# Two GpSimd splits moved behind other work, and a VectorE copy written as a reduce, in an attention and expert kernel

## The chip, the cores and the metric

The kernel runs on one core of a Trainium2 chip. The metric is the device time of one execution in microseconds. TensorE (PE in the profile), VectorE (DVE), ScalarE (ACT) and GpSimd (POOL) each work through their own list of instructions in order; SyncE (SP) and GpSimd issue the transfers.

## The reference

Attention over keys and values that are averaged in groups of 8 rows, and then a layer of experts, in which each row goes through one expert of 8:

```python
k_p = k.reshape(B, H, Sp, 8, D).mean(axis=3)          # B=8, H=8, S=576, D=64, Sp=72
v_p = v.reshape(B, H, Sp, 8, D).mean(axis=3)
attn = softmax(q @ k_p.T / 8)                          # 576 x 72 for each batch and head
x = (attn @ v_p).transpose(0, 2, 1, 3).reshape(B, S, 512)
...
# rows of a batch in order: a row takes its own best expert, or the expert of the row before it
e = argmax(x @ w_gate) if s == 0 or sigmoid(x @ w_local) < 0.5 else prev_e
out[b, s] = softmax(x @ w_gate)[e] * (relu(x[b, s] @ w1[e]) @ w2[e])   # w1 512x1024, w2 1024x512
```

## The kernel before

**Two stages.** The first stage does the attention in 20 units of up to 256 rows (four pairs of batches, five units each), and behind each pair the routing: which expert each row takes (a scan along the rows), and its place in a list of rows for each expert. Attention's rows go to the DRAM tensor `x_rows`, the lists to `ids`. The second stage works through blocks of 256 rows of one expert: it gathers the rows, turns them on TensorE, multiplies by `w1` (eight groups of matmuls for a block) and by `w2`, and scatters the result. Matmuls run on pairs of numbers: each weight is split into a high part (`w1h`, `w2h`: ScalarE's cast, L170 and L175) and a low part (`w1l`, `w2l`: the difference, L171 and L176).

**The order is written by hand.** `PLAN` and `PLAN_B` are lists of short words, each a step with a number; `do` emits the step's instructions. Every engine keeps its instructions in this order, so a step that moves in the list moves past others on each engine that it uses. Words that matter here:

- `w2:c` loads chunk c (a quarter of the 1024x512 `w2`, as 128x1024 numbers) of the most used expert, `p2:c` splits it: a cast on ScalarE (L175), then the difference on GpSimd (L176), or on VectorE where the word is `p2.d`. `p1:c` and `p1.d:c` do the same for `w1` (L170, L171).
- `T0:u`, `T1:u`, `T2:u` turn unit u's attention weights on TensorE (L500) into a buffer of the PSUM pool `ps_t`, which has two; `T0c` and so on copy it out on ScalarE (L354). The routing's transposes (L622) take buffers of the same pool.
- `v0:u` to `v2:u` multiply by the values (L542), `fr`, `fs` scale (L559 to L567), `fp`, `fd` write rows (L580, then a store on SP).
- `rA:n` begins the routing of pair n with small VectorE operations (L598 to L613, `ab` among them), `rT0` to `rT2` turn `ab` (L622), `rS0` to `rS2` scan (L627), `rL` multiplies (L636, L641), `rO` makes the counts (L646 to L650: the line that changes is L649), `rV` the places (L661 to L676).
- `il:0` and `il:1` load a list of rows, `ga:0` and `ga:1` gather them: a sum and a scaling on VectorE (L259, L260), a memset (L262) and two indirect DMAs (L266) on GpSimd. `X0`, `X1` turn the gathered rows (L278) and split them (L285, L286); `L1:n` is a first-layer group (L309, L311) into buffer `hp[n % 3]`, `h0` and `h1` its activation (L316, L317, L321, L322), `L2` the second layer (L333).

Of the kernel before, what the change touches and what calls it, by code (L numbers as in the profile page):

```python
# [12 lines left out]
ALU = mybir.AluOpType  # L13
AX = mybir.AxisListType
# [63 lines left out]
vc:19 v2c:12 ch:0 vm.a:22 fr:12 v0:11 v0c:11 sb:14 vc:20 T0:13 lk:14 v1:11 T0c:13 s:0 s:0 v1c:11 T1:13 v2:11 rR:1 er:0  # L78
T2:13 rV:1 vm.a:18 s:0 sc:15 T1c:13 rP:1 ex:14 T2c:13 vl:19 lq:17 w2:1 fp:12 lq:18 v2c:11 vt:18 kc:15 v0:13 fr:11
vm.a:19 T0:14 mx:15 vd:19 vc:18 T0c:14 s:0 fp:11 w1:3 vl:20 sb:15 vd:20 T1:14 vt:22 v1:13 w1:2 T1c:14 vc:22 vl:18  # L80
fd.p:12 s:0 fd:11 fs:11 lv:23 vd:18 vm.a:21 sc:17 fs:12 vt:21 s:0 kp:14 ex:15 s:0 s:0 v0c:13 p2:1 v1c:13 v2:13 lq:16
s:0 mx:17 sb:17 vc:21 v2c:13 p1.d:3 T0:15 w2:0 v0:14 fr:13 T0c:15 lq:19 vl:21 s:0 T1:15 v0c:14 s:0 fp.d:13 kc:14 T2:15
T1c:15 v1:14 v0:15 fs:13 v1c:14 fd:13 sc:16 fr:14 vd:21 vp.d:23 w1:1 T2c:15 ex:17 s:0 p1:2 fs:14 T0:17 v0c:15 fp:14
w1:0 T1:17 v1:15 vl:22 T0c:17 mx:16 T1c:17 v2:15 fd.p:14 T2:17 v1c:15 sb:16 il:0 vt:23 v0:17 vm.a:23 rA:2 vc:23 T2c:17
sc:18 v2c:15 ex:16 p2:0 fr:15 T0:16 vd:22 mx:18 rT0:2 vl:23 vd:23 rS0:2 v1:17 T0c:16 T1:16 v0c:17 sb:18 v2:17 fp:15
v1c:17 T1c:16 T2:16 rT1:2 fd.p:15 ga:0 fs:15 p1.d:0 v2c:17 fr:17 fp:17 v0:16 rS1:2 T2c:16 sc:19 ex:18 rT2:2 mx:19
v0c:16 rS2:2 v1:16 v1c:16 v2:16 rE:2 sb:19 v2c:16 T0:18 T0c:18 T1:18 rL:2 T2:18 T1c:18 fr:16 fs:17 ex:19 il:1 fd.p:17
fp:16 rO:2 fd:16 v0:18 rR:2 ga:1 T2c:18 fs:16 p1.d:1 X0:0 v0c:18 X0c:0 T0:19 v1:18 v1c:18 T0c:19 v2:18 X1:0 v2c:18
T1:19 rV:2 v0:19 fr:18 X1c:0 T1c:19 v1:19 v0c:19 fs:18 v1c:19
""")  # L90
PLAN_B = plan("""
# [13 lines left out]
def moe_attention(ctx: ExitStack, tc: tile.TileContext, q, q_st, k, v, v_st, w_gate, w1, w2, out):  # L105
    nc = tc.nc
# [230 lines left out]
    with ExitStack() as actx:  # L337
# [254 lines left out]
        state = {"acc": None}  # L592

        def finish(lg, pr):
            def small(name, w, dt=F32):
                return ap2.tile([P, NC, w] if w > 1 else [P, NC], dt, name=name)
# [5 lines left out]
            fr, rs = small("fr", 1), small("rs", 1)  # L602
# [41 lines left out]
            oh, cs = ohs[pr % 2], ap2.tile([P, E, NC + 1], F32, name="cs")  # L644
# [1 line left out]
            nc.vector.tensor_tensor(out=oc, in0=rt[:, 0:NC * E].rearrange("p (c e) -> p c e", e=E),  # L646
                                    in1=iota8[:, 0:1, :].broadcast_to([P, NC, E]), op=ALU.is_equal)
            if pr:
                nc.vector.tensor_copy(out=oh[:, :, 0], in_=state["acc"])  # L649
            nc.vector.tensor_tensor_scan(out=cs.rearrange("p e c -> p (e c)"), data0=seg0.rearrange("p e c -> p (e c)"),  # L650
                                         data1=oh.rearrange("p e c -> p (e c)"), initial=0.0, op0=ALU.mult, op1=ALU.add)
            state["acc"] = cs[:, :, NC]
# [75 lines left out]
        qg, qT, kg, vg, sc, att, fin, rw, tr2, vl = {}, {}, {}, {}, {}, {}, {}, {}, {}, {}  # L728
        first1, first2, lgs, fr = {}, {}, {}, {}
# [12 lines left out]
        def do(name, n):  # L742
# [59 lines left out]
            elif op == "fd":  # L802
                drain(rw[n])
            elif op == "rA":
                fin[n] = finish(lgs[n], n)
                step(fin[n])
            elif op in RSTEPS:
# [403 lines left out]
```

## Time and profile before

| | |
|---|---|
| median of 3 runs | 634.63 us (634.58 to 635.76) |
| the profiled execution | 631.1 us, of which the span 629.4 us |
| TensorE busy | 607.2 us (96%) |
| VectorE busy | 403.6 us (64%) |
| ScalarE busy | 290.8 us (46%) |
| GpSimd busy | 285.2 us (45%) |

All times in the rows below count from the start of the span. An engine's busy share over the whole span says little here: the first stage and the second have different limits, and the change lies where one goes over into the other, at 115 to 160 us.

### The profile page before, as it was taken

The numbers are of one execution on the slowest core, as the hardware profiler recorded it, in microseconds if no ns is written. First come the engines' busy times: TensorE is split into PE (matmuls) and PEld (weight loads), VectorE is DVE, ScalarE is ACT, GpSimd is POOL, SyncE is SP. The second block draws the span as 40 slices with busy tenths as digits, with TensorE's granted clock in tenths as the row PEclk, the third lists the DMA queues.
The fourth block names the chain that finished last, engine by engine and source line by source line (L and its number), as shares of the span: only waits on it lengthen the run. The fifth ranks groups of instructions, "written<-read, shape, count | busy, mean of one in ns | idle before, by whom it ended". The sixth has DMA issues, their size and how long they took to land. (4 is left out here: it accounts for less than half of the span.)

```text
span 629.4 us, 14760 instructions
## 1 busy us (share of the span) xinstructions
PE 607.2 (96%) x3516; PEld 526.8 (84%) x3517; DVE 403.6 (64%) x976; ACT 290.8 (46%) x692; POOL 285.2 (45%) x478
## 2 busy tenths in 40 slices
PE   7999999989999999999999999999999999999992
PEld 6998989878887878888888888888888888888881
DVE  7899899998875515344763585779344494543582
ACT  3677777956432313233642363665132462322550
POOL 5586767875672233203425164426331163132172
PEclk9899999989999999999999999999999999999997
DMA  8998994845102562102542174559121173121011
GB/s 328 348 388 292 346 347 128 314 152 201 20 21 81 172 233 51 50 17 67 167 167 85 27 242 139 153 192 318 50 59 26 42 249 118 34 67 44 24 52 37
DMA packets 53959, 92.00 MB, mean 146 GB/s; under 512 B 30634, under 2 KB 30634, under 8 KB 53932
## 3 DMA queue, kind: packets, MB, share of 16 engines
q1 hardware_dynamic: 45420, 69.61, 33.3%
q0 software_dynamic: 8512, 22.07, 10.3%
q8 instruction: 12, 0.20, 0.1%
q14 instruction: 15, 0.12, 0.1%
HBM read 71.54 MB, written 22.21 MB: 149 GB/s over the span
## 5 line engine op out<-in xcount | busy, mean ns | idle before, releaser
L309 PE MATMUL hp<-x,w1h 128*128 128x512 f32 x364 | 130.4, 399 | 0.1
L333 PE MATMUL o_ps<-w2h,ht_h 128*128 128x512 f32 x312 | 124.0, 397 | 0.0
L333 PE MATMUL o_ps<-w2l,ht_h 128*128 128x512 f32 x312 | 122.0, 391 | 0.0
L311 PE MATMUL hp<-x,w1l 128*128 128x256 f32 x364 | 102.1, 280 | 0.0
L1069 POOL TENSOR_TENSOR vt_in<-idk,zf 128x2 f32<-128x2 f32 x20 | 8.9, 446 | 188.4 <-PE tp L278 178.2
L333 PE MATMUL o_ps<-w2h,ht_l 128*128 128x512 f32 x312 | 87.6, 390 | 0.0
L316 ACT COPY hs<-hp 128x256 f32<-128x256 f32 x91 | 33.5, 371 | 108.4 <-PE hp L311 99.0
L309 PEld LDWEIGHTS hp<-x,w1h 128*128 128x128 f32 x364 | 68.4, 188 | 17.0 <-DVE hs L317 0.4
L1049 DVE TENSOR_SCALAR ob<-o_ps,m_a 128x512 f32<-128x512 f32 x42 | 31.5, 750 | 64.8 <-POOL m_e L1058 30.7
L321 ACT ACTIVATE ht_h<-hs 128x256 fp32r<-128x256 f32 x136 | 57.1, 420 | 29.1 <-DVE hs L317 24.4
L311 PEld LDWEIGHTS hp<-x,w1l 128*128 128x128 f32 x364 | 68.7, 189 | 0.9
L333 PEld LDWEIGHTS o_ps<-w2h,ht_l 128*128 128x128 f32 x312 | 58.6, 188 | 12.8
L333 PEld LDWEIGHTS o_ps<-w2h,ht_h 128*128 128x128 f32 x312 | 58.6, 188 | 11.9
L542 PE MATMUL op<-vaug,aT 128*128 128x148 f32 (+4 forms) x448 | 67.2, 310 | 0.6 <-ACT osb L354 0.6
L333 PEld LDWEIGHTS o_ps<-w2l,ht_h 128*128 128x128 f32 x312 | 58.6, 188 | 10.9
L542 PEld LDWEIGHTS op<-vaug,aT 128*128 128x128 f32 (+1 forms) x448 | 61.2, 182 | 4.0 <-issue 1.3
L322 DVE SCALAR_TENSOR_TENSOR ht_l<-hs,ht_h 128x256 fp32r<-128x256 f32 x136 | 56.6, 418 | 7.4 <-ACT ht_h L321 7.2
L1060 POOL DMA_INDIRECT out<-ob,m_e x42 | 47.8, 1137 | 21.8 <-issue 21.2
L317 DVE TENSOR_TENSOR hs<-hp,hs 128x256 f32<-128x256 f32 x91 | 37.7, 422 | 27.5 <-ACT hs L316 26.2
L285 ACT CAST x<-tp 128x512 fp32r<-128x512 f32 x46 | 24.9, 589 | 52.2 <-PE tp L278 48.4
L302 POOL DMA_INDIRECT vt_in<-x_rows,idk x42 | 41.4, 985 | 12.0 <-issue 8.8
L679 POOL DMA_INDIRECT ids<-pm,pos x36 | 37.5, 1043 | 18.6 <-issue 8.3
(249 smaller groups left out, 1157.4 us busy)
## 6 DMA issues: line engine op xcount, KB each, us to landing
raw<-in_moe_w SPq DMA_DIRECT2D x48, 512.0 KB
kk<-in_k SPq DMA_DIRECT2D x16, 576.0 KB
qt<-in_q SPq DMA_DIRECT2D x16, 512.0 KB
vt_in<-in_v SPq DMA_DIRECT2D x16, 512.0 KB
x_rows<-xs SPq DMA_DIRECT2D x16, 512.0 KB
idp<-ids SPq DMA_DIRECT2D x176, 1.0 KB
vt_in<-in_v_st SPq DMA_DIRECT2D x8, 256.0 KB
vt_in<-in_moe_w SPq DMA_DIRECT2D x4, 512.0 KB
```

The lines of the kernel that those rows point to most:

```text
L302: nc.gpsimd.indirect_dma_start(out=xg[:, h, :], out_offset=None, in_=x_rows[0:NT + 1], in_offset=bass.IndirectOffsetOnAxis(ap=idk[:, h:h + ...
L309: nc.tensor.matmul(out=ps, lhsT=W1[0][:, kk, f * P:(f + 1) * P], rhs=xt[:, kk].rearrange("p i n -> p (i n)"), start=(kk == 0), stop=False, ...
L311: nc.tensor.matmul(out=ps[:, 0:2 * P], lhsT=W1[1][:, kk, f * P:(f + 1) * P], rhs=xt[:, kk, 0, :], start=False, stop=(kk == KD - 1), skip_g ...
L316: nc.scalar.copy(out=hb[:, 0, :], in_=ps[:, 2 * P:])
L317: nc.vector.tensor_tensor(out=hb[:, 1, :], in0=ps[:, 0:2 * P], in1=hb[:, 0, :], op=ALU.add)
L321: nc.scalar.activation(out=ht[0][:, f, :], in_=hb, func=AF.Relu)
L322: nc.vector.scalar_tensor_tensor(out=ht[1][:, f, :], in0=hb, scalar=0.0, in1=ht[0][:, f, :].bitcast(F32), op0=ALU.max, op1=ALU.subtract)
L333: nc.tensor.matmul(out=to[h], lhsT=ht[i][:, kk, h * P:(h + 1) * P], rhs=W2[j][:, kk, :], start=(n == 0), stop=(n == 3 * KF - 1))
L542: nc.tensor.matmul(out=out, lhsT=lhs, rhs=rhs if len(out.shape) == 3 else rhs.rearrange("p s x -> p (s x)"), start=all(x[0] != n for x in ...
L679: nc.gpsimd.indirect_dma_start(out=ids[u % 4].rearrange("t m w -> (t m) w"), out_offset=bass.IndirectOffsetOnAxis(ap=pos[:, u:u + 1], axis=0),
L1049: nc.vector.tensor_scalar(out=ob[:, h, :], in0=o_ps[h], scalar1=m_a[:, h, 1:2], scalar2=None, op0=ALU.mult)
L1060: return nc.gpsimd.indirect_dma_start(out=outv, out_offset=bass.IndirectOffsetOnAxis(ap=m_e[h][:, 0:1], axis=0), in_=ob[:, h, :], in_offse ...
```

## The change

Two words of the list stand elsewhere, and one VectorE instruction is another operation with the same result (a sum over an axis of length 1). The rest of the list is the same, only broken into lines differently.

```diff
-fd.p:12 s:0 fd:11 fs:11 lv:23 vd:18 vm.a:21 sc:17 fs:12 vt:21 s:0 kp:14 ex:15 s:0 s:0 v0c:13 p2:1 v1c:13 v2:13 lq:16
+fd.p:12 s:0 fd:11 fs:11 lv:23 vd:18 vm.a:21 sc:17 fs:12 vt:21 s:0 kp:14 ex:15 s:0 s:0 v0c:13 v1c:13 v2:13 lq:16 s:0
...
-sc:18 v2c:15 ex:16 p2:0 fr:15 T0:16 vd:22 mx:18 rT0:2 vl:23 vd:23 rS0:2 v1:17 T0c:16 T1:16 v0c:17 sb:18 v2:17 fp:15
-v1c:17 T1c:16 T2:16 rT1:2 fd.p:15 ga:0 fs:15 p1.d:0 v2c:17 fr:17 fp:17 v0:16 rS1:2 T2c:16 sc:19 ex:18 rT2:2 mx:19
...
-fp:16 rO:2 fd:16 v0:18 rR:2 ga:1 T2c:18 fs:16 p1.d:1 X0:0 v0c:18 X0c:0 T0:19 v1:18 v1c:18 T0c:19 v2:18 X1:0 v2c:18
...
+sc:18 v2c:15 ex:16 fr:15 T0:16 vd:22 mx:18 rT0:2 vl:23 vd:23 rS0:2 v1:17 T0c:16 T1:16 v0c:17 sb:18 v2:17 fp:15 v1c:17
+T1c:16 T2:16 rT1:2 fd.p:15 p2:0 ga:0 fs:15 p1.d:0 v2c:17 fr:17 fp:17 v0:16 rS1:2 T2c:16 sc:19 ex:18 rT2:2 mx:19 v0c:16
...
+rO:2 fd:16 v0:18 rR:2 ga:1 p2:1 T2c:18 fs:16 p1.d:1 X0:0 v0c:18 X0c:0 T0:19 v1:18 v1c:18 T0c:19 v2:18 X1:0 v2c:18
...
             if pr:
-                nc.vector.tensor_copy(out=oh[:, :, 0], in_=state["acc"])
+                nc.vector.tensor_reduce(out=oh[:, :, 0], in_=state["acc"].unsqueeze(2), axis=AX.X, op=ALU.add)
```

On GpSimd, around the first gather (`qt` is its destination, `xs` a unit's rows), the difference between the two orders reads:

```order
 L171 TENSOR_TENSOR w1l<-kt,w1h 128x1024
 L580 TENSOR_TENSOR xs<-osb,rr 128x256 x2
+L580 TENSOR_TENSOR xs<-osb,rr 128x512 x2
 L176 TENSOR_TENSOR w2l<-vt_in,w2h 128x1024
-L580 TENSOR_TENSOR xs<-osb,rr 128x512 x2
 L262 MEMSET qt 128x1024
 L266 DMA qt<-x_rows,idr_132 128x512 x2
```

The split of chunk 0 has moved past the rows of unit 15 and stands directly ahead of the memset of the first gather.

On GpSimd, behind the second gather, there is now the split of chunk 1, which stood among the scatters of pair 1's lists before:

```order
 L262 MEMSET qt 128x1024
 L266 DMA qt<-x_rows,idr_133 128x512 x2
+L176 TENSOR_TENSOR w2l<-vt_in,w2h 128x1024
 L924 MEMSET zf 128x2
 L924 MEMSET zf_2327 128x1
```

It stands between the second indirect DMA of the gather and the small memsets that open the second stage.

On ScalarE, in the changed kernel, this is the piece with both casts of chunk 1 and of the first-layer chunk behind it (`at` are attention weights, `aT` their copies after the turn, `x_2249` the first block's rows):

```order
L354 COPY aT<-tp 128x512 x2
L484 ACTIVATE at<-ap 128x576
L175 CAST w2h<-vt_in 128x1024
L354 COPY aT<-tp 128x128
L170 CAST w1h<-kt 128x1024
L354 COPY osb<-op 128x444
L285 CAST x_2249<-tp 128x2x256
```

The row L175 is new in this place; before, the exponentials of L484 were followed by the copy of `aT`. The cast of chunk 0 has moved in the same way: from behind the exponentials of unit 16 to behind the copy `T1c` of that unit, where the cast L170 of `p1.d:0` follows it.

## Rows read from the trace of the kernel before

**Rows 1.** The page: TensorE's granted clock in 40 slices, in tenths.

```profile
PEclk9899999989999999999999999999999999999997
```

**Rows 2.** Waits of TensorE, 105 to 205 us: total, times, longest (us).

```profile
PE tp L622 <- DVE ab L607: 1.8, 1, 1.8
PE rt L411 <- DVE vaug L418: 0.8, 1, 0.8
```

**Rows 3.** Windows: us, then PE, PEld, DVE, ACT, POOL busy, clock, DMA share, GB/s.

```profile
130.00:135.00 5.00, 2.92 (x23) 2.10 (x21) 4.76 (x11) 1.68 (x5) 3.46 (x3) 1.00 0.50 158
...
136.00:139.70 3.70, 3.70 (x17) 3.60 (x18) 3.61 (x10) 1.35 (x4) 2.37 (x3) 0.55 0.40 147
```

**Rows 4.** Timeline of VectorE and GpSimd, chunk 0: start us, us, engine, line, instruction.

```profile
131.60 2.33 DVE L607 TENSOR_SCALAR ab<-ab,nz 128x2 f32<-128x2 f32 x1
...
157.32 0.23 DVE L607 TENSOR_SCALAR ab<-ab,nz 128x2 f32<-128x2 f32 x1
...
131.56 2.34 POOL L176 TENSOR_TENSOR w2l<-vt_in,w2h 128x1024 fp32r<-128x1024 f32 x1 [0.44 <-ACT w2h L175]
```

**Rows 5.** Timeline of VectorE and GpSimd, beside the split of chunk 1.

```profile
120.16 2.69 DVE L171 TENSOR_TENSOR w1l<-kt,w1h 128x1024 fp32r<-128x1024 f32 x1
...
119.37 2.39 POOL L176 TENSOR_TENSOR w2l<-vt_in,w2h 128x1024 fp32r<-128x1024 f32 x1
```

**Rows 6.** Timeline of VectorE and GpSimd, around the copy of L649.

```profile
147.64 0.78 DVE L649 COPY oh<-cs 128x8 f32<-128x8 f32 x1
...
149.28 0.17 DVE L259 TENSOR_REDUCE idm<-idn 128x4 f32<-128x16 f32 x1
...
168.09 0.17 DVE L649 COPY oh<-cs 128x8 f32<-128x8 f32 x1
...
147.44 0.95 POOL L262 MEMSET qt<- 128x1024 f32 x1
```

**Rows 7.** Timeline of TensorE, turns of units 16 and 18.

```profile
137.85 1.06 PE L500 MATMUL tp<-ident,at 128*128 128x128 f32 x4
...
145.16 1.03 PE L500 MATMUL tp<-ident,at 128*128 128x128 f32 x8
```

**Rows 8.** Timeline of ScalarE and VectorE, 138 to 145 us.

```profile
138.94 0.59 ACT L354 COPY aT<-tp 128x512 f32<-128x512 f32 x1 [0.33 <-PE tp L500]
139.43 1.05 ACT L170 CAST w1h<-kt 128x1024 fp32r<-128x1024 f32 x1
...
142.02 0.65 DVE L627 TENSOR_TENSOR_SCAN erow<-tp,erow,brow 2x256 f32<-2x256 f32 x1
...
143.07 0.76 DVE L469 TENSOR_REDUCE mx<-sp 128x8 f32<-128x576 f32 x1 [0.40 <-PE sp L454]
...
143.99 0.47 DVE L627 TENSOR_TENSOR_SCAN erow<-tp,erow,brow 2x128 f32<-2x128 f32 x1 [0.17 <-ACT brow L625]
```

**Rows 9.** Timeline of four engines, 147 to 161 us (VectorE: first and last of 43).

```profile
147.49 0.29 DVE L646 TENSOR_TENSOR oh<-rt,iota 128x72 f32<-128x72 f32 x1 [0.55 <-PE rt L641]
...
150.24 1.22 DVE L171 TENSOR_TENSOR w1l<-kt,w1h 128x1024 fp32r<-128x1024 f32 x1
...
153.88 0.63 DVE L286 TENSOR_TENSOR x<-tp,x 128x512 fp32r<-128x512 f32 x1
...
154.43 0.30 DVE L564 TENSOR_TENSOR lgx<-osb,rr 128x144 f32<-128x144 f32 x1
...
159.61 0.75 DVE L317 TENSOR_TENSOR hs<-hp,hs 128x256 f32<-128x256 f32 x2
...
148.48 1.05 ACT L170 CAST w1h<-kt 128x1024 fp32r<-128x1024 f32 x1
...
152.68 1.00 POOL L266 DMA_INDIRECT qt<-x_rows,idr  x1 [0.30 <-DVE sm L662]
...
158.90 1.03 PE L622 MATMUL tp<-ident,ab 128*2 128x128 f32 x8
160.08 0.50 PE L309 MATMUL hp<-x,w1h 128*128 128x512 f32 x1
```

More of the change, by code (lines that the diff above doesn't have):

```diff
@@ L80 @@
 vm.a:19 T0:14 mx:15 vd:19 vc:18 T0c:14 s:0 fp:11 w1:3 vl:20 sb:15 vd:20 T1:14 vt:22 v1:13 w1:2 T1c:14 vc:22 vl:18
-fd.p:12 s:0 fd:11 fs:11 lv:23 vd:18 vm.a:21 sc:17 fs:12 vt:21 s:0 kp:14 ex:15 s:0 s:0 v0c:13 p2:1 v1c:13 v2:13 lq:16
-s:0 mx:17 sb:17 vc:21 v2c:13 p1.d:3 T0:15 w2:0 v0:14 fr:13 T0c:15 lq:19 vl:21 s:0 T1:15 v0c:14 s:0 fp.d:13 kc:14 T2:15
+fd.p:12 s:0 fd:11 fs:11 lv:23 vd:18 vm.a:21 sc:17 fs:12 vt:21 s:0 kp:14 ex:15 s:0 s:0 v0c:13 v1c:13 v2:13 lq:16 s:0
+mx:17 sb:17 vc:21 v2c:13 p1.d:3 T0:15 w2:0 v0:14 fr:13 T0c:15 lq:19 vl:21 s:0 T1:15 v0c:14 s:0 fp.d:13 kc:14 T2:15
 T1c:15 v1:14 v0:15 fs:13 v1c:14 fd:13 sc:16 fr:14 vd:21 vp.d:23 w1:1 T2c:15 ex:17 s:0 p1:2 fs:14 T0:17 v0c:15 fp:14
 w1:0 T1:17 v1:15 vl:22 T0c:17 mx:16 T1c:17 v2:15 fd.p:14 T2:17 v1c:15 sb:16 il:0 vt:23 v0:17 vm.a:23 rA:2 vc:23 T2c:17
-sc:18 v2c:15 ex:16 p2:0 fr:15 T0:16 vd:22 mx:18 rT0:2 vl:23 vd:23 rS0:2 v1:17 T0c:16 T1:16 v0c:17 sb:18 v2:17 fp:15
-v1c:17 T1c:16 T2:16 rT1:2 fd.p:15 ga:0 fs:15 p1.d:0 v2c:17 fr:17 fp:17 v0:16 rS1:2 T2c:16 sc:19 ex:18 rT2:2 mx:19
-v0c:16 rS2:2 v1:16 v1c:16 v2:16 rE:2 sb:19 v2c:16 T0:18 T0c:18 T1:18 rL:2 T2:18 T1c:18 fr:16 fs:17 ex:19 il:1 fd.p:17
-fp:16 rO:2 fd:16 v0:18 rR:2 ga:1 T2c:18 fs:16 p1.d:1 X0:0 v0c:18 X0c:0 T0:19 v1:18 v1c:18 T0c:19 v2:18 X1:0 v2c:18
+sc:18 v2c:15 ex:16 fr:15 T0:16 vd:22 mx:18 rT0:2 vl:23 vd:23 rS0:2 v1:17 T0c:16 T1:16 v0c:17 sb:18 v2:17 fp:15 v1c:17
+T1c:16 T2:16 rT1:2 fd.p:15 p2:0 ga:0 fs:15 p1.d:0 v2c:17 fr:17 fp:17 v0:16 rS1:2 T2c:16 sc:19 ex:18 rT2:2 mx:19 v0c:16
+rS2:2 v1:16 v1c:16 v2:16 rE:2 sb:19 v2c:16 T0:18 T0c:18 T1:18 rL:2 T2:18 T1c:18 fr:16 fs:17 ex:19 il:1 fd.p:17 fp:16
+rO:2 fd:16 v0:18 rR:2 ga:1 p2:1 T2c:18 fs:16 p1.d:1 X0:0 v0c:18 X0c:0 T0:19 v1:18 v1c:18 T0c:19 v2:18 X1:0 v2c:18
 T1:19 rV:2 v0:19 fr:18 X1c:0 T1c:19 v1:19 v0c:19 fs:18 v1c:19
```

## Prediction

> **What bounds the kernel now.** I read the page's busy shares (the table above: TensorE is far ahead of the others) and its row of granted clock first. Its ninth slice of 15.7 us (126 to 142 us) reads 8 where the slices around it read 9: something happens there [rows 1]. A change of order elsewhere counts only where TensorE stands still, or runs slowly after it stood. The view of waits between 105 and 205 us names two such places that touch the change: 1.8 us for `ab` of L607 and 0.8 us for `vaug` of L418, both written by VectorE [rows 2]. The windows show what follows: TensorE has 2.92 us of work in 130 to 135 us, and from 136.0 to 139.7 us the granted clock is 0.55, between the levels of 2.4 and 1.2 GHz and mostly at the lower [rows 3].
>
> The timeline of the two engines says why L607 is late. It is an operation on two columns that takes 0.23 us at 157.32; at 131.60 it takes 2.33 us, and GpSimd's split of second-layer weights (L176, chunk 0) runs from 131.56 to 133.90. It ends 0.03 us after the split [rows 4]. The other split (chunk 1) does the same to VectorE's split of first-layer weights: L171 starts at 120.16, ends at 122.85, 1.09 us after the GpSimd split ended, and takes 2.69 us instead of 1.22 [rows 5, 9]. A VectorE operation of these kinds stands still while a GpSimd split reads SBUF. The copy of L649 is held in the same way by a memset: 0.78 us at 147.64, 0.17 us at 168.09 [rows 6].
>
> **The change part by part.** *Chunk 0 leaves L607.* The waits of 1.8 and 0.8 us go [rows 2], and with them the slow clock: 3.70 us x (1 - 0.55) = 1.7 us [rows 3]. That is 4.3 us, and the most the change can give.
>
> *Its new place.* The split follows ScalarE's cast of chunk 0, which now stands behind the copy of TensorE's transposes T1 of unit 16 and ahead of a first-layer cast. I count from TensorE's start of these transposes (137.85 now). At full clock they take about 0.55 us (1.06 at half clock [rows 7]), the copy 0.59, the cast 1.05 as its neighbour does [rows 8], the GpSimd split 2.34 [rows 4]: it ends near 4.6 us. VectorE's split L171 needs the next cast (3.2) and reads two SBUF tensors as it did at 120 us, so it waits until 4.6; then come 1.22 us of its own [rows 9], 0.28 us to the scan L627 and 0.65 us of scan [rows 8]: 6.8 us. That scan frees the PSUM buffer which the transposes of unit 18 take. TensorE reaches them 145.16 - 137.85 = 7.3 us after the start now, 0.9 us of it due to the half clock until 139.7, so after 6.4 us: a new wait of 0.4 us. The second four of those transposes need the buffer that the last scan frees, 0.76 + 0.47 us later (8.0) [rows 8]; the first four are done by about 7.3: another 0.7 us. Together 1.1 us, at least 0 (if VectorE gets in first) and at most 1.3 (all steps late by the gaps between rows). I take 1.1, since both buffers are needed in this order.
>
> *Chunk 1 leaves its old place.* VectorE's L171 at 120 us gets 1.5 us shorter [rows 5]. TensorE does not wait there, so this is worth nothing by itself; it makes VectorE early at 131 us. But GpSimd's queue moves up by the split's 2.4 us too, and with it the first-layer split that it does before chunk 0; there that one can hold the small operations of VectorE that stand ahead of L607. Then some of the 0.8 us at L418 stays. Bounds 0 and 0.8; I take 0.2, since VectorE is ahead by most of that.
>
> *Chunk 1's new place,* behind the second gather. Here VectorE sets the time. From L646 (147.49), which waits for TensorE, to the add L317 (159.61), 43 rows follow each other with no gap over 0.17 us, and TensorE's next matmul (160.08) needs the buffer that L317 reads, with its transposes at 158.90 needing VectorE's rows just ahead [rows 9]. So whatever is added to VectorE in this stretch, TensorE waits for. Three things happen. The reduce in L649's place takes 0.17 us, as a reduce of 16 elements does, against 0.78 [rows 6]: -0.6 us (0 if it is held like the copy; I take the small row). ScalarE now casts chunk 1 (1.05 us) ahead of the cast that VectorE's L171 at 150.24 waits for. That cast started at 148.48 and lasted 1.05 us; it now ends at 150.58, so L171 is 0.34 us later than before, and the 0.6 us is spent in this wait. Then GpSimd's split starts when the second gather has been issued: 152.68 + 1.00 = 153.68 before, and up to 0.34 later now, with L171 beside the first issue. It runs until about 156.4. VectorE's first operation behind it with two SBUF inputs is L564 (154.43 before); it would go on at 156.4, 2.0 us late, the 0.34 included [rows 9]. Bounds: 0.3 us (nothing is held) and 2.6 (0.34 and one whole split of 2.34). I take 2.0, by the case of L171 at 120 us.
>
> The Trainium skill, "SBUF — State Buffer", section "Who interferes with whom", says that a VectorE instruction with two SBUF inputs and a GpSimd instruction that reads SBUF exclude each other for a whole instruction, that the one which starts first wins, and that tensor_reduce never contends on this chip. The trace agrees on the first point (L171 stands until GpSimd's split has ended, 122.85 against 121.76 plus 1.09). By its last point the reduce is never held and costs its 0.17 us; no row shows a reduce beside a memset, and by the other bound, 0.78 us, the sum would be the same, because the later cast of ScalarE covers the difference down to 0.34 us.
>
> *Costed at nothing.* The other copies of L649 lie where no other operation holds them (0.17 us at 168.09 [rows 6]). The order of transfers stays as it is; behind the two late loads of second-layer weights on SP's queue stand only row stores, and neither load waits for chunk 1. The second-layer matmuls that read chunks 0 and 1 stand in the written order behind eight first-layer groups (L1:0 to L1:7), so both splits are in time; if that cover were gone, each would cost its 2.34 us.
>
> **Sum.** 4.3 - 1.1 - 0.2 - 2.0 = 1.0 us gained. The profiled execution took 631.1 us (span 629.4 and 1.7 around it), which would become 630.1. The median of the runs shown is 634.63, 3.5 us above the profiled one; I take the same microsecond off it: 633.6. About 0.2% (1.3 us) is what a measurement of this kernel can tell from no change, so this forecast is just inside.
>
> **The rivals.** *A, as summed:* the old stall goes, two smaller ones come: 633.6, give or take 0.9. Chance 0.40.
>
> *B, the clock falls again.* TensorE would wait about 1.6 us at 158.90 and 0.4 us at 160.08 after the change. The drop at 136 us followed 1.8 and 0.8 us. If 2.0 us are enough, another 1.7 us go at half clock and 635.2 results. For it: the same shape of stall. Against it: 2.0 us are less than 2.6, and no row shows a stall in between. Chance 0.20.
>
> *C, chunk 1 does not hold VectorE.* VectorE gets in between the gather and the split, or the split starts where only PSUM operands follow (L286 lies there). Then only 0.3 us are lost: 4.3 - 1.1 - 0.2 - 0.3 = 2.7 gained, 631.9. For it: the hold is a matter of tenths of a microsecond in start times. Against it: after L286 every second row of VectorE reads two SBUF tensors. Chance 0.22.
>
> *D, both new places are free:* the full 4.3 us, 630.3. It needs L171 ahead of a split that precedes its own cast. Chance 0.06.
>
> *E, slower:* the split in the new place catches VectorE ahead of the x split L286 (153.88). L286 then ends about 2 us late, the first-layer matmuls that need it stand still, the wait at L317 is 2.6 us, the clock falls (1.7 us) and only 3.0 us were won before: 3.0 - 2.6 - 1.7 = -1.3 us, 635.9; with the upper bound of the first part (1.3) and of the second (0.8) 636.7. The point that decides is a start of the split ahead of about 153.3 us in the time of before. Chance 0.12.
>
> **How the numbers follow.** Faster by over 0.2% (below 633.4): C, D and three tenths of A, 0.40. Within 0.2%: nearly all the rest of A and two thirds of B, 0.39. Slower: E, a third of B and a little of A, 0.21. The predicted time is A's. The range reaches from D (630.3) to E (636.4) and leaves out a part of both.
>
> **What would show it.** Right: no wait at L607 and full clock at 136 to 140 us; a wait of transposes L500 for the scan L627 near 141; VectorE's L564 (or a neighbour) stretched to 1.5 to 2.3 us beside L176 near 152, and TensorE waiting at L622 and at the fourth first-layer group. Wrong: L564 and its neighbours at their 0.2 to 0.3 us (C or D), a stretched row ahead of L286 (E), half clock near 160 us (B), or a wait for the gathered rows at L278, whose gather is issued behind chunk 0 here.

## The result, and the profile after

The changed kernel took 639.4 us (median), the kernel before 635.8 us in the same comparison: ratio 1.0063, 95% interval 1.0041 to 1.0084, so 3.6 us slower where 1.0 us faster was foreseen. One run of 1013 us, in which the granted clock was 0.557, is left out. Two later comparisons of the same two kernels gave 1.0018 (1.0000 to 1.0036) and 1.0018 (1.0002 to 1.0035), 1.1 us each, with intervals from nothing to 2.3 us. All three comparisons point the same way: the change makes the kernel slower by about a microsecond. The rest of the first 3.6 us did not come again.

From here on, all fences hold rows of the kernel that the sentence ahead names. First, two rows of the changed kernel's page: busy time by engine and the granted clock in 40 slices.

```profile
PE 607.1 (95%) x3516; PEld 524.2 (82%) x3517; DVE 403.5 (63%) x976; ACT 290.9 (46%) x692; POOL 282.8 (44%) x478
PEclk9999999989999999999999999999999999999997
```

The waits of TensorE in the changed kernel, 105 to 205 us (total, times, longest), which answer to [rows 2]:

```profile
PE op L542 <- ACT osb L354: 3.5, 1, 3.5
PE hp L309 <- DVE x L286: 1.2, 1, 1.2
...
PE hp L309 <- DVE hs L317: 0.8, 1, 0.8
...
PE tp L500 <- DVE erow L627: 0.4, 1, 0.4
PE rt L656 <- DVE oh L649: 0.4, 1, 0.4
```

Its windows, which answer to [rows 3] (columns as there):

```profile
120.00:125.00 5.00, 1.99 (x21) 1.18 (x17) 4.88 (x9) 1.79 (x4) 3.75 (x4) 0.97 0.63 238
125.00:130.00 5.00, 3.62 (x13) 3.48 (x14) 2.61 (x10) 4.14 (x10) 0.00 (x0) 0.50 0.61 201
...
135.00:140.00 5.00, 5.00 (x41) 4.68 (x39) 3.73 (x18) 2.68 (x9) 2.00 (x2) 1.00 0.29 70
```

And rows of its timeline (start, us, engine, line, operation, and in brackets the idle time before it and what ended it), which answer to [rows 4 to 9]:

```profile
122.42 1.28 DVE L171 TENSOR_TENSOR w1l<-kt,w1h 128x1024 fp32r<-128x1024 f32 x1
125.80 0.53 ACT L354 COPY osb<-op 128x444 f32<-128x444 f32 x1 [4.01 <-issue]
136.18 0.23 DVE L607 TENSOR_SCALAR ab<-ab,nz 128x2 f32<-128x2 f32 x1
139.11 0.60 PE L622 MATMUL tp<-ident,ab 128*2 128x128 f32 x4
142.40 0.17 DVE L260 TENSOR_SCALAR idr<-idm 128x2 int32<-128x2 f32 x1
143.49 2.37 POOL L176 TENSOR_TENSOR w2l<-vt_in,w2h 128x1024 fp32r<-128x1024 f32 x1 [3.44 <-ACT w2h L175]
144.39 2.55 DVE L171 TENSOR_TENSOR w1l<-kt,w1h 128x1024 fp32r<-128x1024 f32 x1 [1.15 <-ACT w1h L170]
149.45 2.05 POOL L580 TENSOR_TENSOR xs<-osb,rr 128x512 f32<-128x512 f32 x2
149.49 2.06 DVE L559 TENSOR_SCALAR rr<-osb 128x16 f32<-128x16 f32 x1
152.50 0.16 DVE L649 TENSOR_REDUCE oh<-cs 128x8 f32<-128x8 f32 x1
157.63 2.90 DVE L666 TENSOR_TENSOR pm<-pv,sm 128x9 f32<-128x9 f32 x1 [0.17 <-DVE pv L665]
158.10 2.39 POOL L176 TENSOR_TENSOR w2l<-vt_in,w2h 128x1024 fp32r<-128x1024 f32 x1
160.89 0.63 DVE L286 TENSOR_TENSOR x<-tp,x 128x512 fp32r<-128x512 f32 x1
161.57 0.50 PE L309 MATMUL hp<-x,w1h 128*128 128x512 f32 x1 [1.24 <-DVE x L286]
```

Read from the top: the old stall is gone (L607 takes 0.23 us, L622 has no wait, the clock from 135 to 140 us is 1.00). Chunk 0's split stands beside L171, which takes 2.55 us, as foreseen. Not foreseen is the next pair: GpSimd's two row multiplications (L580) hold the small L559 for 2.06 us. Chunk 1's split holds L666 for 2.90 us, ahead of L286, and TensorE waits for L286. And there is a row that has to do with none of this: at 121.8 us ScalarE stands for 4.01 us with nothing in the profile that it waits for ("issue"), TensorE waits 3.5 us for it at L542 and goes on at a clock of 0.50.

**How far each stretch reaches.** The same four TensorE rows can be found in every trace. In the second trace of the changed kernel they are these (the two L500 are the last rows ahead of the first and of the second transposes L622; L278 is the second turn of gathered rows; L309 the fourth first-layer group):

```profile
130.95 0.60 PE L500 MATMUL tp<-ident,at 128*128 128x128 f32 x4
...
134.71 0.27 PE L500 MATMUL tp<-ident,at 128*128 128x128 f32 x1
...
150.33 0.66 PE L278 MATMUL tp<-ident,qt 128*128 128x128 f32 x4 [0.30 <-ACT aT L354]
...
160.53 0.50 PE L309 MATMUL hp<-x,w1h 128*128 128x512 f32 x1 [0.87 <-DVE hs L317]
```

Their differences are three stretches: A (the old stall), B (chunk 0's new place), C (chunk 1's). "Start" is where A begins; it differs by 7.7 us from execution to execution.

| kernel (trace) | start | A | B | C | A+B+C |
|---|---|---|---|---|---|
| before | 131.56 | 8.44 | 12.11 | 7.97 | 28.52 |
| before, again | 135.76 | 7.36 | 12.11 | 7.96 | 27.43 |
| changed | 138.67 | 3.77 | 14.41 | 10.19 | 28.37 |
| changed, again | 130.95 | 3.76 | 15.62 | 10.20 | 29.58 |
| changed, third | 133.16 | 3.83 | 16.47 | 9.34 | 29.64 |

The change wins 3.5 to 4.7 us in A, loses 2.3 to 4.4 in B and 1.4 to 2.2 in C. Of the 8.4 us by which the first two profiles differ (637.8 against 629.4 us of span), 7.1 lie ahead of A and 1.4 behind C.

The three stretches are not the whole kernel. What follows C takes 468.9 to 472.3 us in the seventeen traces of this document: 468.9 to 469.3 in five (before; changed, again and third; chunk 0 alone; chunk 1 on VectorE), 470.0 or more in the others, eight of which have weight loads at L333 waiting 1.2 to 1.6 us in all for VectorE's L176 and four a chunk put off (below). Both kernels are in both groups. So a time can fail to show what A, B and C gain.

### The profile page after: what moved, and what is told of

The parts are those of the page before. It is cut to its first block, busy times and chain, and to the rows that moved or that the text cites. A ratio compares the mean times of both kernels' runs of the same rounds, so it can differ in the third digit from the quotient of the medians.

```text
span 637.8 us, 14761 instructions
## 1 busy us (share of the span) xinstructions
PE 607.1 (95%) x3516; PEld 524.2 (82%) x3517; DVE 403.5 (63%) x976; ACT 290.9 (46%) x692; POOL 282.8 (44%) x478
## 4 chain that ended last, share of the span: by engine, by line
PE 61%; POOL 0%; issue 0%; DVE 0%; POOLq 0%; DVEq 0%
PE o_ps L333 28%; PE hp L309 10%; PE hp L311 5%; PE hp L945 4%; PE tp L309 4%; PE tp L278 3%; PE tp L311 2%; PE rt L309 2%; PE rt L311 1%; PE rt L951 0%; PE hp L951 0%; POOL out L1060 0%; DVE ob L1049 0%; POOLq L1207 0%; POOL zf L1059 0%
## 5 line engine op out<-in xcount | busy, mean ns | idle before, releaser
L309 PE MATMUL hp<-x,w1h 128*128 128x512 f32 x364 | 130.6, 399 | 2.0 <-DVE x L286 1.2
L333 PE MATMUL o_ps<-w2h,ht_h 128*128 128x512 f32 x312 | 124.0, 397 | 0.0
L333 PE MATMUL o_ps<-w2l,ht_h 128*128 128x512 f32 x312 | 122.2, 392 | 0.8 <-DVE w2l L176 0.6
L333 PE MATMUL o_ps<-w2h,ht_l 128*128 128x512 f32 x312 | 87.7, 390 | 0.0
L309 PEld LDWEIGHTS hp<-x,w1h 128*128 128x128 f32 x364 | 68.4, 188 | 19.2 <-DVE x L286 1.6
L542 PE MATMUL op<-vaug,aT 128*128 128x148 f32 (+4 forms) x448 | 67.3, 309 | 4.2 <-ACT osb L354 4.2
L333 PEld LDWEIGHTS o_ps<-w2h,ht_l 128*128 128x128 f32 x312 | 58.6, 188 | 12.6
L333 PEld LDWEIGHTS o_ps<-w2l,ht_h 128*128 128x128 f32 x312 | 58.6, 188 | 12.6 <-DVE w2l L176 1.6
L333 PEld LDWEIGHTS o_ps<-w2h,ht_h 128*128 128x128 f32 x312 | 58.6, 188 | 11.9
L542 PEld LDWEIGHTS op<-vaug,aT 128*128 128x128 f32 (+1 forms) x448 | 61.0, 181 | 7.7 <-ACT osb L354 4.5
L322 DVE SCALAR_TENSOR_TENSOR ht_l<-hs,ht_h 128x256 fp32r<-128x256 f32 x136 | 56.5, 417 | 6.3 <-ACT ht_h L321 5.3
L317 DVE TENSOR_TENSOR hs<-hp,hs 128x256 f32<-128x256 f32 x91 | 37.7, 422 | 29.8 <-ACT hs L316 27.2
```

The lines of the kernel that those rows point to most:

```text
L309: nc.tensor.matmul(out=ps, lhsT=W1[0][:, kk, f * P:(f + 1) * P], rhs=xt[:, kk].rearrange("p i n -> p (i n)"), start=(kk == 0), stop=False, ...
L317: nc.vector.tensor_tensor(out=hb[:, 1, :], in0=ps[:, 0:2 * P], in1=hb[:, 0, :], op=ALU.add)
L322: nc.vector.scalar_tensor_tensor(out=ht[1][:, f, :], in0=hb, scalar=0.0, in1=ht[0][:, f, :].bitcast(F32), op0=ALU.max, op1=ALU.subtract)
L333: nc.tensor.matmul(out=to[h], lhsT=ht[i][:, kk, h * P:(h + 1) * P], rhs=W2[j][:, kk, :], start=(n == 0), stop=(n == 3 * KF - 1))
L542: nc.tensor.matmul(out=out, lhsT=lhs, rhs=rhs if len(out.shape) == 3 else rhs.rearrange("p s x -> p (s x)"), start=all(x[0] != n for x in ...
```

## Experiments

**The kernel before, again; and each move taken back or done alone.** No edit in the first; in the others, of the two moved words:

```diff
(chunk 1 in its old place, chunk 0 moved, reduce kept)
-ga:1 p2:1 T2c:18        v0c:13 v1c:13
+ga:1 T2c:18             v0c:13 p2:1 v1c:13
(of the kernel before, chunk 1 alone moved)
-v0c:13 p2:1 v1c:13      ga:1 T2c:18
+v0c:13 v1c:13           ga:1 p2:1 T2c:18
(of the kernel before, chunk 0 alone moved)
-ex:16 p2:0 fr:15        fd.p:15 ga:0
+ex:16 fr:15             fd.p:15 p2:0 ga:0
```

> The kernel before, unchanged, profiled and timed once more. The changed kernel's trace shows 8.4 us more span than the first trace of before, but its timed median is only about 3.6 us above. Theory 'rare gap in before' : the first trace of before is a lucky execution, and this one is near 634 us with a ScalarE or TensorE gap of 3 to 5 us that the first trace does not have. Rival, 'the change alone': this trace is near 631 us again, without any such gap, and TensorE's wait for VectorE at L607 (1.8 us) is the only large one between 105 and 160 us.

> The changed kernel with the split of chunk 1 back in its old place; chunk 0's move and the reduce stay. Theory 'early gap': ScalarE's gap of 4.0 us that ends at 125.8 us comes from taking chunk 1's cast out of the early stretch, so here it is gone, the half clock of 125 to 135 us too, and of the waits at 160 to 167 us (1.24 and 0.80) nothing is left: about 4.3 - 1.1 = 3 us faster than before. Rival 'new places': the gap has another cause (chunk 0's place or the reduce) and stays; then only the 2.0 us of the waits at 160 to 167 us and a little clock go, and the kernel is 1 to 2 us slower than before.

> The kernel before with the split of chunk 1 alone moved behind the second gather. Theory 'early gap': ScalarE's gap of about 4 us near 122 to 126 us is here too, with half clock behind it, and the waits at L309 of 1.2 and 0.8 us near 160 us; the wait at L607 stays or is absorbed in the gap: 3 to 6 us slower than before. Rival 'new places': no gap near 125 us, only about 2 us of waits near 160 us: 1 to 2 us slower.

> The kernel before with chunk 0's split alone moved (ahead of the first gather); chunk 1 and the copy as before. By the prediction's terms: 4.3 us gained at L607 and 1.1 lost near 141 us, so about 3 us faster. Rival 'the stall is absorbed': what is gained at 130 to 140 us is the 3.2 us that the changed kernel's trace shows against before from 129 to 139 us, and from 139 to 160 us 1.7 us are lost as in the version with chunk 1 in its old place: 1.5 us gained at most, which does not show clearly.

| | ratio to before (95%) | start | A | B | C | A+B+C |
|---|---|---|---|---|---|---|
| before, again | 0.9982 (0.9955 to 1.0008) | 135.76 | 7.36 | 12.11 | 7.96 | 27.43 |
| chunk 1 old, chunk 0 moved, reduce | 0.9997 (0.9976 to 1.0018) | 135.28 | 3.81 | 15.29 | 7.96 | 27.06 |
| chunk 1 alone moved | 1.0005 (0.9979 to 1.0030) | 135.15 | 5.69 | 13.27 | 10.19 | 29.15 |
| chunk 0 alone moved | 1.0020 (1.0004 to 1.0037) | 132.49 | 4.07 | 17.75 | 7.94 | 29.76 |

Single times of the kernel before run from 630.7 to 639.2 us in the comparison of the first three rows, so the times tell little. None of the three moves differs from before by as much as was expected (chunk 0 alone, foreseen 3 us faster, is 1.3 us slower by its ratio; in its B the copy of L649 takes 1.43 us and the clock falls, to 0.81 over the stretch). The stretches tell more: C is 7.94 to 7.96 us with chunk 1 in its old place and 10.19 with it moved, and A falls to about 4 us when chunk 0 is moved. The trace of before again begins A 4.2 us later than the first one. About 1.2 us of this went behind a gap of ScalarE at 107 us (1.88 us, "issue"), 0.7 at L500 near 122 us, and 2.5 at L448, which waited for L472 of VectorE:

```profile
127.53 3.13 DVE L564 TENSOR_TENSOR lgx<-osb,rr 128x72 f32<-128x72 f32 x1
127.63 2.37 POOL L171 TENSOR_TENSOR w1l<-kt,w1h 128x1024 fp32r<-128x1024 f32 x1
129.94 1.19 POOL L580 TENSOR_TENSOR xs<-osb,rr 128x256 f32<-128x256 f32 x2
133.69 2.23 PE L448 MATMUL sp<-kdz,qt 128*128 128x144 f32 x16 [2.47 <-DVE ap L472]
```

This is a hold as well: L564, which stands ahead of L472, takes 3.13 us beside GpSimd's first-layer split, where in the first trace it took 0.23 at 126.23, ahead of that split. VectorE came 1.3 us later, and the hold made it 4.2. So the kernel before has gaps of ScalarE too; its first trace has none of 0.6 us or more between 105 and 131 us. The theory that they come from taking chunk 1's cast away falls: with chunk 1 moved alone there is a gap of 1.19 us near 107 and none of 4 us at 122.

**The changed kernel with a tiny ScalarE operation in the old place of the cast.**

```diff
-v0c:13 v1c:13
+v0c:13 na:0 v1c:13
+            elif op == "na":
+                nc.scalar.activation(out=warm_act, in_=ones[:, 0:1], func=AF.Copy)
```

> The changed kernel with one tiny ScalarE operation (a copy of one column) where the cast of chunk 1 used to stand, so that ScalarE's list has as many instructions ahead of 120 us as before. Theory 'ScalarE waits for its code': the gap depends on where a refill of the instruction list falls, so it goes away or is shorter, and the kernel is about 4 us faster than the changed one. Rival 'something that the cast or the GpSimd split does there': the gap of 4.0 us stays at 125 us, and the time is the changed kernel's within 0.3 us.

Ratio 1.0022 (0.9996 to 1.0048); no gap at 122 us, A 3.77, B 14.40, C 10.21 us. By itself that spoke for the count of instructions. The next run took it back.

**The changed kernel, again and a third time.** No edit.

> The changed kernel, unchanged, once more. The kernel before repeated gave single times from 630.7 to 639.2 us, while the changed one gave 638.9 to 639.7. Theory 'early gap is the change': ScalarE's gap of 4 us near 122 us comes back in the profile, and the median is near 639 us, 3 us above before. Rival 'early gap is an accident of one series': the gap is absent or elsewhere, single times spread over 5 us or more as for the others, and the median is 1 us or less above before.

> The changed kernel a third time, beside the version with chunk 0 put off. The prediction said 1.0 us faster; the first comparison gave 3.6 us slower, the second 1.2. Theory 'holds alone': from 131 to 160 us the profile again loses about 5.7 us (3.5 for chunk 0's place, 2.2 for chunk 1's) against 4.7 won, no ScalarE gap of 4 us near 122 us, and the median is 1 to 2 us above before. Rival 'an early gap belongs to the change': a gap of ScalarE of 3 us or more between 117 and 130 us is there again, and the median is over 3 us above before.

Medians 631.66 against 630.44 us and 632.33 against 630.74 us, with no gap over 0.8 us of ScalarE between 105 and 131 us in either trace. The gap of 4 us did not come again, so nothing shows it to be part of the change. The third trace has B at 16.47 us because the clock fell there: 0.66 from 145 to 150 us, after 3.24 us of TensorE work in 140 to 145. The clock also fell in B of chunk 1 on VectorE (0.89 over the stretch) and of chunk 1 put off (0.88), both below.

VectorE and GpSimd in the second trace, in B:

```profile
135.67 0.18 DVE L259 TENSOR_REDUCE idm<-idn 128x4 f32<-128x16 f32 x1 [1.12 <-DMA idn<-ids]
135.76 2.37 POOL L176 TENSOR_TENSOR w2l<-vt_in,w2h 128x1024 fp32r<-128x1024 f32 x1 [2.49 <-ACT w2h L175]
135.89 3.16 DVE L260 TENSOR_SCALAR idr<-idm 128x2 int32<-128x2 f32 x1
138.06 0.96 POOL L262 MEMSET qt<- 128x1024 f32 x1
138.07 0.97 DVE L564 TENSOR_TENSOR lgx<-osb,rr 128x144 f32<-128x144 f32 x1
...
142.94 2.05 POOL L580 TENSOR_TENSOR xs<-osb,rr 128x512 f32<-128x512 f32 x2
...
143.19 1.83 DVE L559 TENSOR_SCALAR rr<-osb 128x16 f32<-128x16 f32 x1
```

GpSimd's operations hold VectorE's in turn: the split and the memset behind it hold L260 (it ends at 139.05, the memset at 139.02), the row multiplications behind the gathers hold L559. L564 ends with L260; whether the memset holds it too, or only L260 ahead of it, the rows do not tell. Ahead of the hold VectorE waited 1.12 us at L259 for the load of the list. By these rows the wait decides which row the split catches: in the first trace of the changed kernel there was none, L260 was through at 142.40, 1.1 us ahead of the split, and the split caught L171.

In the first trace of the kernel before, the last pair stands like this:

```profile
142.63 2.06 POOL L580 TENSOR_TENSOR xs<-osb,rr 128x512 f32<-128x512 f32 x2
...
145.87 0.17 DVE L559 TENSOR_SCALAR rr<-osb 128x16 f32<-128x16 f32 x1 [0.75 <-ACT osb L354]
```

There L559 comes when both multiplications have ended, 14.3 us after the start of A against 12.2 here, and is free.

**The changed kernel with chunk 1's difference on VectorE, in its new place.**

```diff
-ga:1 p2:1 T2c:18
+ga:1 p2.d:1 T2c:18
```

> The changed kernel with the difference of chunk 1 on VectorE in the same new place, so that GpSimd splits nothing there. Theory 'it is the hold': VectorE's L666 (2.90 us in the changed kernel) is short again, but 1.2 us of the split itself stand ahead of L286, so the wait of 1.24 us at L309 falls to about 0.3 and that of 0.80 stays at most as it is: 1 us faster than the changed kernel. Rival 'VectorE's time counts, whoever fills it': no change, since 1.2 us of work and the cast of ScalarE ahead of it replace a hold of 2.7 us in which the other work was only put off.

Ratio 0.9997 (0.9982 to 1.0013). C is 7.97 us again and L666 takes 0.17 us: the 2.2 us in C are the hold. What the 1.2 us of the difference cost in B, where they now stand on VectorE, cannot be read from its 15.81 us, since the clock fell there. By C both expectations were too low, 2.2 us instead of 1 or none; the time fell by 0.5 us (631.15 against 631.66 of the changed kernel in the same comparison).

**Chunk 1, then chunk 0, put off into the second stage.** All three are edits of the changed kernel; the third has chunk 1 as there and chunk 0 put off.

```diff
(chunk 1 put off)
-ga:1 p2:1 T2c:18        h0:4 h1:3 L1:5
+ga:1 T2c:18             h0:4 h1:3 p2.d:1 L1:5
(chunk 0 put off, chunk 1 in its old place)
-fd.p:15 p2:0 ga:0       h0:4 h1:3 L1:5           ga:1 p2:1 T2c:18    v0c:13 v1c:13
+fd.p:15 ga:0            h0:4 h1:3 p2.d:0 L1:5    ga:1 T2c:18         v0c:13 p2:1 v1c:13
(chunk 0 put off, chunk 1 as in the changed kernel)
-fd.p:15 p2:0 ga:0       h0:4 h1:3 L1:5
+fd.p:15 ga:0            h0:4 h1:3 p2.d:0 L1:5
```

> The changed kernel with the whole split of chunk 1 (cast and difference, this on VectorE) put off into the second stage, ahead of the sixth first-layer group, where VectorE and ScalarE are busy 60% and 45% of the time. Theory 'new place of chunk 1': between 140 and 160 us the 3.4 us lost by the changed kernel shrink to the 1.7 us that chunk 0's place costs, the waits of 1.24 and 0.80 us at L309 are gone, and the kernel is about 2 to 3 us faster than the changed one and level with before or 1 us faster. Rival: the time only moves, since second-layer matmuls wait for chunk 1 or VectorE's first-layer work is late by the 1.2 us: the changed kernel's time within 1 us.

> Chunk 1 in its old place, the reduce kept, and chunk 0's whole split put off into the second stage, ahead of the sixth first-layer group, with its difference on VectorE. So GpSimd has no split left between 130 and 160 us. Theory 'GpSimd's queue behind the split': the split alone takes 2.4 us there, and it pushes the memset, two gather issues and two row multiplications of 1.0 us beside VectorE's later rows, which then stand (L564 0.97, L559 1.83 us in the repeated trace of the changed kernel). Without it L260, L564 and L559 take 0.2 to 0.3 us, the gain of 4.7 us at 131 to 140 us is kept but for 1 us, and the kernel is about 3 us faster than before. Rival 'VectorE or ScalarE sets the time anyway' (GpSimd's two row multiplications hold L559 wherever they fall, or chunk 0 is late for the second layer): 1 us faster or none.

> The version with chunk 1 in its old place, chunk 0 put off into the second stage and the reduce, a second time on another chip. If the 3.4 us of the first comparison are real, it is 2 to 4 us faster than before again and 3 to 5 us faster than the changed kernel beside it; if they were an accident, within 1 us of before.

> As the version with chunk 0 put off, but chunk 1 behind the second gather as in the changed kernel. It shows chunk 1's new place with nothing of chunk 0 around it. Theory: VectorE's L666 is held for 2.9 us ahead of L286, TensorE waits 1.2 and 0.8 us at L309, so 2.2 us slower than the version with chunk 1 in its old place. Rival: chunk 1's hold only mattered because chunk 0 had made VectorE late: then under 0.7 us.

| | ratio to before (95%) | start | A | B | C | A+B+C |
|---|---|---|---|---|---|---|
| chunk 1 put off | 1.0015 (0.9993 to 1.0036) | 133.70 | 3.77 | 14.66 | 7.96 | 26.39 |
| chunk 0 put off, chunk 1 old | 0.9953 (0.9928 to 0.9978) | 133.34 | 3.76 | 13.29 | 7.94 | 24.99 |
| the same, again | 0.9984 (0.9968 to 1.0000) | 133.62 | 3.76 | 13.35 | 7.97 | 25.08 |
| chunk 0 put off, chunk 1 as changed | 1.0012 (0.9997 to 1.0027) | 131.77 | 3.77 | 13.50 | 10.20 | 27.47 |

With chunk 0 put off and chunk 1 in its old place the kernel is faster than both: 1.0 to 3.0 us below before by the two ratios (the second interval ends at 1.0000), and 2.5 us below the changed kernel in the comparison that has both (629.80 against 632.33 us). Chunk 1's hold alone costs 1.9 us there (631.69 against 629.80), 2.2 by C. With chunk 1 put off, C is free of the hold too, but the time is the changed kernel's (631.99 against 631.66 us), not 2 to 3 us less as expected. VectorE and GpSimd in B, chunk 0 put off, chunk 1 old (first trace):

```profile
138.85 0.18 DVE L259 TENSOR_REDUCE idm<-idn 128x4 f32<-128x16 f32 x1 [1.51 <-DMA idn<-ids]
139.06 0.17 DVE L260 TENSOR_SCALAR idr<-idm 128x2 int32<-128x2 f32 x1
139.14 0.30 DVE L564 TENSOR_TENSOR lgx<-osb,rr 128x144 f32<-128x144 f32 x1
...
143.32 2.05 POOL L580 TENSOR_TENSOR xs<-osb,rr 128x512 f32<-128x512 f32 x2
143.57 1.84 DVE L559 TENSOR_SCALAR rr<-osb 128x16 f32<-128x16 f32 x1
```

L260 and L564 are free, L559 is still held. TensorE's rows in B say where the time goes. The first trace of before has L636 6.12 and the first L278 9.17 us behind the end of A; the others come later by (us):

| | at L636 | from there to the first L278 | from there on | B's loss |
|---|---|---|---|---|
| changed | 1.0 | 0.9 | 0.4 | 2.3 |
| changed, again | 2.4 | 0.7 | 0.4 | 3.5 |
| chunk 0 moved, chunk 1 old, reduce | 2.4 | 0.7 | 0.1 | 3.2 |
| chunk 0 put off, chunk 1 old | 0.4 | 0.7 | 0.1 | 1.2 |

So of what the changed kernel loses in B, about 1.2 us have nothing to do with the split's new place. VectorE, freed of the stall at L607, first waits for the load of the list (1.51 us at L259), and TensorE waits for its scan at L500: 0.4. Then it runs into GpSimd's row multiplications, and TensorE comes to L656 and L657 behind the held L559: 0.7. This is read from the rows; no run moves these multiplications or that load. The last 0.4 us of the changed kernel are a wait of L278 for ScalarE's copy `aT`, which is absent where chunk 1 is in its old place. My expectation missed the hold: it had L559 free too. Putting the chunk off is not free either: TensorE waits 0.4 to 0.7 us at L333 for L322 of VectorE, 1.4 us where chunk 1 is moved as well.

**Chunk 0's difference on VectorE, in its new place** (chunk 1 in its old place).

```diff
-fd.p:15 p2:0 ga:0       ga:1 p2:1 T2c:18    v0c:13 v1c:13
+fd.p:15 p2.d:0 ga:0     ga:1 T2c:18         v0c:13 p2:1 v1c:13
```

> Chunk 1 in its old place, the reduce kept, chunk 0 in its new place but with the difference on VectorE. Theory 'GpSimd's queue behind the split': GpSimd comes to the memset, the gathers and the row multiplications 2.4 us earlier, VectorE pays 1.2 us for the difference, and between 140 and 152 us about 1.5 us are lost instead of the 3.2 us of the version with GpSimd's split; 1.5 to 3 us faster than before. Rival 'only the place counts': 3 us lost again, level with before within 1 us.

B is 13.66 us, against 15.29 with GpSimd's split in the same place: the 1.2 us of VectorE's work cost 0.3 us more than no split at all, GpSimd's 2.4 us cost 1.9. The time does not show it: ratio 1.0001 (0.9974 to 1.0028), where 1.5 to 3 us were expected. In the trace A begins at 136.79, 5.2 us behind the first trace of before, 2.5 of them by the same hold of L564 as in the trace of before again (3.14 us).

**The reduce alone, and the changed kernel with the copy.**

```diff
(of the kernel before)
-                nc.vector.tensor_copy(out=oh[:, :, 0], in_=state["acc"])
+                nc.vector.tensor_reduce(out=oh[:, :, 0], in_=state["acc"].unsqueeze(2), axis=AX.X, op=ALU.add)
```

> The kernel before with the reduce in place of the copy, nothing else. The prediction's price: L649 takes 0.16 instead of 0.78 us at 147.6, so VectorE's chain to L317 is up to 0.6 us earlier, and TensorE, which waits there, too: 0 to 0.6 us faster. Rival: a reduce that stands beside GpSimd's memset or row multiplication is held like the copy: no change, with a row of 0.7 us or more.

> The changed kernel with the copy kept. In the version with chunk 0 alone moved the copy of L649 took 1.43 us beside GpSimd's row multiplication and memset, in the changed kernel the reduce took 0.15 us. Theory 'the reduce is never held': the copy takes 1.0 to 1.5 us here, the first transposes of the gathered rows come about 1.2 us later, and the kernel is 0.5 to 1.5 us slower than the changed one, about 2 us slower than before on a chip where the changed one is 1 us slower. Rival: the cast of chunk 1 on ScalarE is what VectorE waits for next, as the prediction had it, and covers the difference: the changed kernel's time.

The kernel before with the reduce alone, beside GpSimd's memset:

```profile
149.26 0.95 POOL L262 MEMSET qt<- 128x1024 f32 x1
...
149.46 0.16 DVE L649 TENSOR_REDUCE oh<-cs 128x8 f32<-128x8 f32 x1
```

The changed kernel with the copy:

```profile
147.43 1.04 POOL L580 TENSOR_TENSOR xs<-osb,rr 128x512 f32<-128x512 f32 x1 [0.46 <-issue]
...
147.97 1.42 DVE L649 COPY oh<-cs 128x8 f32<-128x8 f32 x1
...
148.41 0.95 POOL L262 MEMSET qt<- 128x1024 f32 x1
...
149.81 0.44 PE L657 MATMUL rt<-cs,ones 128*128 128x72 f32 x2 [1.21 <-DVE cs L650]
```

The reduce is not held where the copy is. In the changed kernel it is worth 1.1 us of B (16.71 with the copy, 15.62 without) and the ratio with the copy is 1.0029 (1.0004 to 1.0053). In the kernel before it is worth nothing in the trace (A+B+C 27.38 against 27.43 of before again), while its time was lower, ratio 0.9968 (0.9939 to 0.9997). No row accounts for these 2 us, so this stays inconclusive.

## Why the prediction was wrong, step by step

- **Chunk 0 leaves L607: right.** Foreseen 4.3 us less 0.2; A falls by 4.7 against the first trace of before and by 3.6 against its second, where the stall was smaller. Full clock and L607 at 0.23 us came as said.
- **"Its new place", 1.1 us: the step that failed.** It followed VectorE's L171 behind the split, and TensorE's wait at L500 for the scan (0.4 to 1.2 us) is there; in the first trace, where the split caught L171 as foreseen, the loss up to L636 is 1.0 us. But it counted one hold, and only as far as the scan. Measured for the whole of B: 2.3, 3.5 and 4.4 us. Three things were left out. VectorE, which comes to the last L559 2.0 to 3.5 us earlier than in the first trace of before, counted from the start of A, waits for the list in the second and third trace (1.12 and 0.52 us at L259), so that the split catches L260 instead, and the loss up to L636 is 2.4 us. GpSimd's own queue goes on behind the split: the memset, two gather issues and two row multiplications, which hold L559 (0.7 to 0.9 us of TensorE). And ScalarE's cast of chunk 1 delays a copy (0.4). With chunk 0 put off 1.2 us are lost, with GpSimd's split in the new place 2.0 more (13.29 against 15.29 in B). The third trace agrees with the second to 0.01 us at L636 and then loses 0.9 more, by the clock. With chunk 0 alone moved, and the copy, the clock fell too, to 0.59 from 145 to 150 us: rival B's mechanism, in another place.
- **The reduce:** foreseen at 0.17 us, with 0.6 us against the copy that ScalarE's later cast would cover. It took 0.16, and the cast covered nothing here: 1.1 us in the changed kernel, since the copy would have been held by L580 and the memset for 1.42 us.
- **Chunk 1 leaves its old place, nothing by itself: right.** L171 takes 1.28 us instead of 2.69 and no row shows a gain. The 0.2 us set against it do not show either: in the first two traces of the changed kernel TensorE works through the whole of A (3.77 of 3.77 and 3.76 of 3.76 us).
- **Chunk 1's new place, 2.0 us: right in size, wrong in the row.** 2.2 us in C in two traces of the changed kernel (10.2 against 7.96), 1.4 in the third. The split catches L666 ahead of L286, rival E's mechanism, at about the point that was named (158.10 less the 4.7 us by which TensorE is late there is 153.4). TensorE waits 1.24 us for L286 and 0.80 for L317. The clock, which E let fall near 160 us, stayed at 1.00 in C; in the third trace it fell in B instead.
- **The sum:** with 3.5 us in B (the middle one of three traces) in place of 1.1 the prediction's own terms give 4.3 - 3.5 - 0.2 - 2.0 = -1.4 us, slower by 1.4, against 1.1 in the two repeated comparisons; with 2.3 or 4.4 it would be slower by 0.2 or 2.3. Two slips in the rivals change nothing: B's sum is 635.3, not 635.2, and the 636.4 given as E's end of the range is neither of E's two sums (635.9, 636.7).
- **The 3.6 us of the first comparison:** no term covers them. 4.0 us of ScalarE standing at 122 us are in that trace alone. What ScalarE waited for stays open. In that trace a packet of the queue that the page of the profile lists as q14, instruction, lands between 125.25 and 125.50 us, just ahead of the gap's end at 125.80; but each of the other traces has one such packet between 122.5 and 127.5 us without such a gap, and no instruction packet stands beside the gaps near 106 us. Adding an instruction made no difference that the plain repeat did not show as well, and gaps of 0.6 to 1.9 us near 106 us stand in ten of the seventeen traces, in one of the two of the unchanged kernel too.

## What to carry to other kernels

When a stall goes, ask what the freed engine meets next: here VectorE came 2 to 4 us earlier, waited for the load of a list and stood behind GpSimd's row multiplications, so a part was given back with no further cause. When an operation is moved on GpSimd, write down the whole piece of its queue behind the new place, with times, and lay it beside VectorE's rows; here one hold came with others. Where single times of one kernel spread over 5 us or more and the change is worth one, cut the traces at the same rows and compare the stretches; and look at what lies behind the last cut too, before a gain in a stretch is called a gain in time.

## What the runs showed of the hardware

- Executions of one kernel came to the same TensorE row, L500 ahead of L622, at 131.56 and 135.76 us. The differences arise between 105 and 131 us, a stretch in which loads run (in the first trace of before the DMA share is 1.02 to 1.04 from 110 to 120 us): in gaps of ScalarE with no visible cause (0.6 to 4.0 us), in waits at L448 for a query load (0.2 to 1.8 us in six traces), and in holds that VectorE meets only when it comes a little later (L564, 3.13 us instead of 0.23 behind a delay of 1.3 us). The medians of the kernel before were 630.4 to 636.2 us in five comparisons.
- In the profile a held row can start ahead of the GpSimd row that it is due to: L666 starts at 157.63, the split at 158.10, and they end at 160.53 and 160.49. Without the split L666 takes 0.17 us in the same place, beside the same gather issue (151.50 with chunk 0 put off and chunk 1 old).
- The Trainium skill, "SBUF — State Buffer", section "Who interferes with whom", says that tensor_reduce never contends on this chip and that a copy can. The runs agree: 0.16 us beside a memset, where the copy takes 0.78 [rows 6] and, beside a multiplication and a memset, 1.42 us.
- A small operation is held as long as a large one: L260, which writes two columns, stood 3.16 us beside a split of 2.37 and the memset of 0.96 behind it. And GpSimd need not read anything for a hold: the copy of L649 beside a memset alone took 0.78 us, 0.17 elsewhere [rows 6].
